# Attention scaled on VectorE behind both maxima, with transposed copies moved to ScalarE

## The chip, the cores and the metric

The kernel runs on one core of one Trainium2 chip. TensorE multiplies and transposes, VectorE (DVE in the rows), ScalarE (ACT) and GpSimd (POOL) work on rows of 128 partitions, SyncE (SP) issues most DMAs. Each engine takes its instructions in the order in which the program lists them, and waits at one whose inputs or buffers aren't ready. The metric is the device time of one execution in microseconds (us); less is better.

## What is computed

The reference runs attention and then two feed-forward blocks over its output, all in float32:

```
scores = q @ k.T / sqrt(64) + bias(i, j)       # 4 batches, 8 heads, 576 tokens, 64 per head
attn   = exp(scores - max(scores))             # rows of 576
attn   = attn / (sum(attn) + 1e-9)
x      = (attn @ v), heads side by side        # 2304 tokens x 512
x      = moe(x):  h = x @ w_in;  (h * cos(h)) @ w_out                       # width 2048
out    = moe2(x): rms norm, then (silu(xn @ w_gate) * (xn @ w_val)) @ w_out # width 1536
```

The bias is a small two-layer network of the distance of two tokens; it depends on the head and not on the batch.

## The kernel before

**Stages.** In the traced execution the first 64 us build the bias, attention follows to 357 us, and the two feed-forward blocks fill the rest. Their matrices arrive as 64-bit words and are taken apart on the chip.

**Units and steps.** Attention runs in 16 units: one batch and two heads each. A unit `u` has five steps `p`: steps 0 to 3 take 128 queries of both heads, step 4 the last 64 of both. The order in which `step(u, p)` writes its parts is the order of every engine's queue. A step holds:

- `qk(u, p)`: the scores into PSUM tiles `psS` (two buffers, so that it waits for the maxima of the step before).
- `softmax`: per head one VectorE instruction (L334, "maximum" below) that adds the bias, writes the sums to `e` and their extreme to `sm`, then ScalarE's exponential (L338), which also leaves the row sum. `sums` (L343, ScalarE) adds the 1e-9.
- `scale(u, p-1)`: the exponentials of the step before times the reciprocal of their sum: L350 is the reciprocal on VectorE, L353 one instruction of 128x576 for each head (one in step 4). After step 4's, L355 copies 64 columns on GpSimd.
- `tr(u, p-2)`: TensorE transposes the exponentials of two steps before into PSUM tiles `pt` (three buffers). For p < 4 there are two large tiles (four transposes, copied to `eT` by L367) and a small one (L371). Step 4 has one large and one small tile, copied by L377 and L380, L381.
- `av`: TensorE's products of `eT` with `v` (L393), for the unit before. They go to the one PSUM buffer `o`, which is emptied by L404 (ScalarE, the part `xh`) and L405 (VectorE, the remainder `xl`); the next `av` into `o` waits for L405. This happens at steps 0 and 2.

From unit 5 on the work on the first feed-forward matrices is mixed in: at step 1 L114 and L115 on VectorE, at step 4 L118 and L119 (a piece of a matrix is one such pair and the other), at step 0 L135 and L103 on ScalarE and L136 on GpSimd.

After the last unit, `scale(15, 4)` stands ahead of the first two items of the feed-forward part, inside which the last transposes and products run.

Of the kernel before, what the change touches and what calls it, by code (L numbers as in the profile page):

```python
# [11 lines left out]
ALU = mybir.AluOpType  # L12
# [3 lines left out]
B, H, S, D = 4, 8, 576, 64  # L16
# [29 lines left out]
def attn_moe(tc, qd, kd, vd, smallp, lrow, ident_d, wf1, wf2, rmsg, out):  # L46
    nc = tc.nc
# [137 lines left out]
    def load_bias(hp, j, eng=nc.sync):  # L185
        if hp >= NHP:
            return
        t = prep.tile([128, S], F32, tag=f"bias{j}", name=f"bias{j}", bufs=1)
        if j < 8:
            qt, hh = divmod(j, 2)  # L190
            eng.dma_start(
                t, bflat[2 * hp + hh, 128 * qt * ROW:128 * (qt + 1) * ROW]
                .rearrange("(p r) -> p r", r=ROW)[:, 16:16 + S])
        else:

            for p0, c0, c1, k0 in ((0, 0, S, 0), (64, 0, S - 64, 64), (64, S - 64, S, 0)):
                eng.dma_start(
                    t[p0:p0 + 64, c0:c1],
                    bflat[2 * hp + p0 // 64, 512 * ROW:576 * ROW]
                    .rearrange("(p r) -> p r", r=ROW)[:, 16 + k0:16 + k0 + c1 - c0])  # L200
        bias_t[j] = t
# [108 lines left out]
    def qk(u, p):  # L310


        kt, qt_ = kq[u]
        if p < 4:
            pss = [psB.tile([128, 2, 512], F32, tag="S", name="psS", bufs=2) for _ in range(2)]
            for x in range(2):
                for hh in range(2):
                    r = slice(64 * hh, 64 * hh + 64)
                    k0 = 64 - 64 * hh + 288 * x
                    nc.tensor.matmul(pss[hh][:, x, 0:288], qt_[r, 128 * p:128 * p + 128], kt[r, k0:k0 + 288],  # L320
                                     start=True, stop=True, tile_position=(64 * hh, 0))
            return pss
        ps = psB.tile([128, 2, 512], F32, tag="S", name="psS", bufs=2)
        for x in range(2):
            nc.tensor.matmul(ps[:, x, 0:288], qt_[:, 512:640], kt[:, 64 + 288 * x:352 + 288 * x], start=True, stop=True)  # L325
        return [ps]

    def softmax(u, j, ps):
        s_ = st[u]
        if j % 2 == 0:  # L330
            s_["e"][j // 2] = ep.tile([128, 2 * S], F32, tag="e", name="e", bufs=4)
        e2 = s_["e"][j // 2]
        e = e2[:, S * (j % 2):S * (j % 2) + S]
        nc.vector.tensor_tensor_reduce(  # L334
            out=e.rearrange("p (a b) -> p a b", a=2), in0=ps[:, :, 0:288],
            in1=bias_t[j].rearrange("p (a b) -> p a b", a=2),
            scale=-0.125, scalar=3.0e38, op0=ALU.add, op1=ALU.min, accum_out=s_["m"][:, j:j + 1])
        nc.scalar.activation(e, e, AF.Exp, bias=s_["m"][:, j:j + 1], scale=-1.0, accum_out=s_["sum"][:, j:j + 1])  # L338

    def sums(u, p):  # L340
        s_ = st[u]
        a, z = (2 * p, 2 * p + 2) if p < 4 else (8, 9)
        nc.scalar.activation(s_["sum"][:, a:z], s_["sum"][:, a:z], AF.Identity, bias=tiny)  # L343

    def scale(u, p):

        s_ = st[u]
        e2 = s_["e"][p]
        a, z = (2 * p, 2 * p + 2) if p < 4 else (8, 9)
        nc.vector.reciprocal(s_["r"][:, a:z], s_["sum"][:, a:z])  # L350
        for j in range(a, z):
            e = e2[:, S * (j % 2):S * (j % 2) + S]
            nc.gpsimd.tensor_tensor(e, e, s_["r"][:, j:j + 1].to_broadcast([128, S]), op=ALU.mult)  # L353
        if p == 4:
            nc.gpsimd.tensor_copy(e2[:, S:S + 64], e2[:, S - 64:S])  # L355

    def tr(u, p):
        s_ = st[u]
        e = s_["e"].pop(p)
        if p < 4:  # L360
            eT, q0 = (s_["eT0"], 128 * p) if p < 2 else (s_["eT1"], 128 * (p - 2))
            for c, ev in ((0, nc.scalar.copy), (2, nc.vector.tensor_copy)):
                pt = psA.tile([128, 512], F32, tag="tr", name="pt", bufs=3)
                for i in range(4):
                    k0 = 128 * (c + i // 2) + (S + 64) * (i % 2)
                    nc.tensor.transpose(pt[:, 128 * i:128 * i + 128], e[:, k0:k0 + 128], ident)  # L366
                ev(eT[:, 2 * c:2 * c + 4, q0:q0 + 128], pt.rearrange("p (c q) -> p c q", c=4))  # L367

            pt = psA.tile([128, 512], F32, tag="tr", name="pt", bufs=3)
            nc.tensor.transpose(pt[:, 0:128], e[:, 512:640], ident)  # L370
            nc.vector.tensor_copy(eT[:, 8, q0:q0 + 128], pt[:, 0:128])  # L371
        else:
            eT = s_["eT1"]
            pt = psA.tile([128, 512], F32, tag="tr", name="pt", bufs=3)
            for c in range(4):
                nc.tensor.transpose(pt[:, 128 * c:128 * c + 128], e[:, 128 * c:128 * c + 128], ident)
            nc.scalar.copy(eT[:, 0:8, 256:320], pt.rearrange("p (c q) -> p c q", c=8))  # L377
            pt = psA.tile([128, 512], F32, tag="tr", name="pt", bufs=3)
            nc.tensor.transpose(pt[:, 0:128], e[:, 512:640], ident)
            nc.vector.tensor_copy(eT[0:64, 8, 256:320], pt[0:64, 0:64])  # L380
            nc.vector.tensor_copy(eT[64:128, 8, 256:320], pt[64:128, 64:128])  # L381

    def av(u, half, cs):
        s_ = st[u]
        n = 256 if half == 0 else 320
        eT = s_["eT0"] if half == 0 else s_["eT1"]
        if cs[0] == 0:
            s_["o"] = psA.tile([128, 512], F32, tag="o", name="o", bufs=1)
        o = s_["o"]
        vt = vts[u]  # L390
        for c in cs:
            for hh in ((0, 1) if c % 2 else (1, 0)):
                nc.tensor.matmul(o[64 * hh:64 * hh + 64, 0:n], vt[:, c, 64 * hh:64 * hh + 64],  # L393
                                 eT[:, 2 * c + (hh if c < 4 else 0), :], start=(c == 0), stop=(c == 4),
                                 tile_position=(0, 64 * hh))

    def o_out(u, half):

        hp, b = divmod(u, 4)
        n = 256 if half == 0 else 320  # L400
        o = st[u]["o"][:, 0:n]
        t0 = b * S + 256 * half
        h, l = xh[:, hp, t0:t0 + n], xl[:, hp, t0:t0 + n]
        return [lambda: nc.scalar.copy(h, o),  # L404
                lambda: nc.vector.tensor_tensor(l, o, h.bitcast(F32), op=ALU.subtract)]  # L405

    def start_unit(u):
        hp, b = divmod(u, 4)
        vt = ap.tile([128, 5, 128], F32, tag="v", name="v", bufs=2)
        nc.sync.dma_start(vt, vd[b, hp])  # L410
        vts[u] = vt
        sm = ap.tile([128, 32], F32, tag="sm", name="sm", bufs=2)
        st[u] = {
            "m": sm[:, 0:9], "sum": sm[:, 10:19], "r": sm[:, 20:29], "e": {},
        }

    def step(u, p):
        hp, b = divmod(u, 4)
        if p == 0:
            start_unit(u)  # L420
        if u == 0 and p == 0:
            for j in (6, 7, 8):
                load_bias(0, j)
        outs = o_out(u - 2, 1) if p == 0 and u > 1 else o_out(u - 1, 0) if p == 2 and u > 0 else []
        for f in outs[:1]:
            f()
        pss = qk(u, p)
        if u or p:
            scale(*((u, p - 1) if p else (u - 1, 4)))
        for j, ps in enumerate(pss, 2 * p):  # L430
            softmax(u, j, ps)
            if b == 3:
                load_bias(hp + 1, j)
            if j % 2 == 0:
                for f in outs[1:]:
                    f()
        sums(u, p)
        if p == 2:
            st[u]["eT0"] = ap.tile([128, 9, 256], F32, tag="eT0", name="eT0", bufs=1)
        if p == 4:  # L440
            if u > 0:
                av(u - 1, 1, [4])
            st[u]["eT1"] = ap.tile([128, 9, 320], F32, tag="eT1", name="eT1", bufs=1)
        if p > 1:
            tr(u, p - 2)
        elif u > 0:
            tr(u - 1, p + 3)
        if u > 0 and p < 4:
            av(u - 1, *((0, [0, 1, 2]), (0, [3, 4]), (1, [0, 1]), (1, [2, 3]))[p])
        if p == 1 and u > 0:  # L450
            load_k(u + 1)
            load_q(u + 1)
        if u >= 4 and p in (1, 4):
            w_fill()
        if u >= 4 and p == 0:
            w_tick(lambda i: i < WA + WB)

    for u in range(16):
        for p in range(5):
            step(u, p)  # L460
# [329 lines left out]
```

## Time and profile before

| | |
|---|---|
| time, median of 3 runs (lowest to highest) | 1226.73 us (1226.02 to 1226.89) |
| time of the profiled execution | 1223.5 us |
| its span, first to last instruction | 1221.6 us |
| granted clock of TensorE, mean over the span | 0.997 |
| busy, share of the span | TensorE 96%, VectorE 69%, ScalarE 45%, GpSimd 40% |

The rows are those of the profiled execution, whose own time is 1.9 us above its span; it was 3.2 us faster than the median of the other runs. A busy time is the sum of an engine's instructions; "idle before" names what an engine waited for. Where two instructions of an engine overlap by their ends, their starts are further apart than nothing but nearer than their durations: starts are what a queue is counted by.

### The profile page before, as it was taken

What the parts mean: (1) busy time and instruction counts of PE and PEld (TensorE: products, weight loads), DVE (VectorE), ACT (ScalarE), POOL (GpSimd) and SP (SyncE); (2) the same over time, 40 slices, a digit from 0 to 9 for tenths busy, and PEclk for the clock granted to TensorE, in tenths of its full rate; (3) what the DMA queues carried; (4) which work ended last, traced back from release to release, by engine and by line L of the source; (5) the groups of instructions that cost most, each with busy time, mean ns of one, the idle gap of its engine ahead of it and who ended that gap; (6) DMA issues with size and microseconds to landing.
All of it is one profiled execution on the core that took longest, in us unless ns stands there. A gap on an engine that the chain in (4) does not pass through costs nothing.

```text
span 1221.6 us, 17077 instructions
## 1 busy us (share of the span) xinstructions
PE 1171.7 (96%) x6276; PEld 895.6 (73%) x6276; DVE 839.1 (69%) x1607; ACT 551.2 (45%) x1121; POOL 491.8 (40%) x471
## 2 busy tenths in 40 slices
PE   7889998888899999999999999999999999999998
PEld 2355555555567878888888887878888888888887
DVE  8866678777767869979888989687456255633232
ACT  6866776676655345444534545532232132212111
POOL 4155565665653225224424435674341232124111
PEclk9989999999999999999999999999999999999999
DMA  5922416143111101111110100121011111200012
GB/s 153 306 92 87 166 52 185 62 142 122 62 46 35 53 1 52 52 35 35 52 53 18 57 31 18 40 64 52 18 53 54 34 35 52 69 1 1 35 38 84
DMA packets 30323, 79.24 MB, mean 65 GB/s; under 512 B 3872, under 2 KB 4128, under 8 KB 30240
## 3 DMA queue, kind: packets, MB, share of 16 engines
q1 hardware_dynamic: 29616, 76.09, 19.7%
q0 software_dynamic: 480, 1.77, 0.6%
q8 instruction: 50, 0.82, 0.3%
q10 hardware_dynamic: 144, 0.29, 0.1%
q14 instruction: 33, 0.27, 0.1%
HBM read 62.52 MB, written 15.61 MB: 64 GB/s over the span
## 4 chain that ended last, share of the span: by engine, by line
PE 75%; DVE 15%; ACT 4%; issue 4%; DMA 1%; POOL 0%; DVEq 0%; ACTq 0%; POOLq 0%
PE y L499 24%; PE h L499 13%; PE hg L499 11%; PE hv L499 11%; PE o L393 6%; PE psS L320 4%; PE pt L366 3%; DVE e L334 3%; DVE ft L254 2%; PE psS L325 2%; PE psb L283 1%; DVE w L118 1%; DVE xl L405 1%; DVE w L114 1%; DVE t L539 1%
## 5 line engine op out<-in xcount | busy, mean ns | idle before, releaser
L499 PE MATMUL y<-g,wB 128*128 128x512 f32 (+1 forms) x960 | 213.6, 370 | 3.9 <-DVE yacc L594 1.7
L353 POOL TENSOR_TENSOR e<-e,sm 128x576 f32<-128x576 f32 x144 | 164.1, 1159 | 108.8 <-DVE sm L350 69.0
L547 POOL TENSOR_TENSOR g<-t,g 128x512 fp32r<-128x512 f32 (+1 forms) x80 | 97.5, 1219 | 245.8 <-ACT g L546 245.8
L499 PEld LDWEIGHTS y<-g,wB 128*128 128x128 f32 x960 | 167.5, 189 | 37.2 <-DVE yacc L594 3.0
L558 POOL TENSOR_TENSOR g<-t,g 128x512 fp32r<-128x512 f32 (+1 forms) x60 | 74.4, 1241 | 291.9 <-ACT g L557 291.9
L338 ACT ACTIVATE e<-e,sm 128x576 f32<-128x576 f32 x144 | 111.1, 772 | 93.7 <-DVE sm L334 91.6
L499 PE MATMUL h<-xh,wB 128*128 128x512 f32 (+1 forms) x480 | 145.8, 369 | 0.0
L499 PE MATMUL y<-wB,g 128*128 128x512 f32 x594 | 143.5, 389 | 0.0
L499 PE MATMUL hv<-xh,wB 128*128 128x512 f32 (+1 forms) x440 | 133.7, 369 | 0.0
L499 PE MATMUL hg<-xh,wB 128*128 128x512 f32 (+1 forms) x440 | 133.2, 368 | 0.4 <-DVE t L553 0.4
L334 DVE CUSTOM_DVE_ANT_0 e<-psS,bias 128x576 f32<-128x576 f32 x144 | 105.9, 753 | 39.6 <-PE psS L320 23.1
L553 DVE TENSOR_TENSOR t<-t,hg 128x512 f32<-128x512 f32 (+1 forms) x60 | 38.0, 633 | 137.4 <-ACT t L552 137.4
L499 PEld LDWEIGHTS y<-wB,g 128*128 128x128 f32 x594 | 110.8, 188 | 22.5
L393 PE MATMUL o<-eT,v 128*64 128x256 f32 (+1 forms) x640 | 94.6, 417 | 17.7 <-DVE xl L405 17.7
L552 ACT ACTIVATE t<-hg 128x512 f32<-128x512 f32 (+1 forms) x60 | 33.3, 556 | 167.9 <-PE hg L499 161.6
L557 ACT CAST g<-t 128x512 fp32r<-128x512 f32 (+1 forms) x60 | 34.7, 578 | 164.5 <-DVE t L556 164.5
L543 ACT ACTIVATE r<-r 128x512 f32<-128x512 f32 (+1 forms) x80 | 47.1, 589 | 127.4 <-DVE r L540 127.0
L499 PEld LDWEIGHTS h<-xh,wB 128*128 128x128 f32 x480 | 87.7, 188 | 16.2 <-POOL wB L136 0.7
L136 POOL TENSOR_TENSOR wB<-w,wB 128x512 fp32r<-128x512 f32 x61 | 85.5, 1408 | 19.6 <-ACT wB L135 19.6
L499 PEld LDWEIGHTS hg<-xh,wB 128*128 128x128 f32 x440 | 80.5, 188 | 15.0 <-DVE t L553 0.9
L499 PEld LDWEIGHTS hv<-xh,wB 128*128 128x128 f32 x440 | 80.6, 189 | 13.7
L499 PE MATMUL h<-xl,wB 128*128 128x512 f32 (+1 forms) x240 | 88.4, 368 | 0.0
(113 smaller groups left out, 2150.0 us busy)
## 6 DMA issues: line engine op xcount, KB each, us to landing
raw<-in_wf_dram SPq DMA_DIRECT2D x68, 512.0 KB, 3.6
bflat<-G SPq DMA_DIRECT2D x36, 295.5 KB, 4.0
bias<-bflat SPq DMA_DIRECT2D x26, 288.0 KB, 3.2
kt<-in_kd_dram SPq DMA_DIRECT2D x16, 320.0 KB, 4.6
qt<-in_qd_dram SPq DMA_DIRECT2D x16, 320.0 KB, 4.9
v<-in_vd_dram SPq DMA_DIRECT2D x16, 320.0 KB, 2.9
out_dram<-yacc SPq DMA_DIRECT2D x16, 256.0 KB, 2.1
bias<-bflat POOLq DMA_DIRECT2D x6, 288.0 KB, 5.6
```

The lines of the kernel that those rows point to most:

```text
L136: eng.tensor_tensor(t[:, 1, :], r, t[:, 0, :].bitcast(F32), op=ALU.subtract)
L320: nc.tensor.matmul(pss[hh][:, x, 0:288], qt_[r, 128 * p:128 * p + 128], kt[r, k0:k0 + 288], start=True, stop=True, tile_position=(64 * hh, 0))
L334: nc.vector.tensor_tensor_reduce(out=e.rearrange("p (a b) -> p a b", a=2), in0=ps[:, :, 0:288], in1=bias_t[j].rearrange("p (a b) -> p a b" ...
L338: nc.scalar.activation(e, e, AF.Exp, bias=s_["m"][:, j:j + 1], scale=-1.0, accum_out=s_["sum"][:, j:j + 1])
L353: nc.gpsimd.tensor_tensor(e, e, s_["r"][:, j:j + 1].to_broadcast([128, S]), op=ALU.mult)
L366: nc.tensor.transpose(pt[:, 128 * i:128 * i + 128], e[:, k0:k0 + 128], ident)
L393: nc.tensor.matmul(o[64 * hh:64 * hh + 64, 0:n], vt[:, c, 64 * hh:64 * hh + 64], eT[:, 2 * c + (hh if c < 4 else 0), :], start=(c == 0), s ...
L499: nc.tensor.matmul(ps, a, b_, start=(first and k == 0), stop=(last and k == tot - 1))
L543: nc.scalar.activation(r, r, AF.Abs)
L547: nc.gpsimd.tensor_tensor(g[:, 1, :tn], t, g[:, 0, :tn].bitcast(F32), op=ALU.subtract)
L553: nc.vector.tensor_tensor(t, t, pg, op=ALU.mult)
L558: nc.gpsimd.tensor_tensor(g[:, 1, :tn], t, g[:, 0, :tn].bitcast(F32), op=ALU.subtract)
```

## The change

It does three things. The two multiplications of `scale` go from GpSimd (`tensor_tensor` with the reciprocal broadcast) to VectorE (`tensor_scalar` with one value per partition). `scale(u, p-1)` is written behind both maxima of step `p` rather than ahead of them. And of the copies of transposed tiles, ScalarE takes the small one of every `tr` with p < 4 and the second large one of p = 2; in a unit that is four small ones and one of the four large ones that VectorE had.

```diff
@@ scale
         nc.vector.reciprocal(s_["r"][:, a:z], s_["sum"][:, a:z])
         for j in range(a, z):
             e = e2[:, S * (j % 2):S * (j % 2) + S]
-            nc.gpsimd.tensor_tensor(e, e, s_["r"][:, j:j + 1].to_broadcast([128, S]), op=ALU.mult)
+            nc.vector.tensor_scalar(e, e, s_["r"][:, j:j + 1], None, op0=ALU.mult)
@@ tr
-            for c, ev in ((0, nc.scalar.copy), (2, nc.vector.tensor_copy)):
+            for c, ev in ((0, nc.scalar.copy), (2, nc.scalar.copy if p == 2 else nc.vector.tensor_copy)):
...
             nc.tensor.transpose(pt[:, 0:128], e[:, 512:640], ident)
-            nc.vector.tensor_copy(eT[:, 8, q0:q0 + 128], pt[:, 0:128])
+            nc.scalar.copy(eT[:, 8, q0:q0 + 128], pt[:, 0:128])
@@ step
         pss = qk(u, p)
-        if u or p:
-            scale(*((u, p - 1) if p else (u - 1, 4)))
         for j, ps in enumerate(pss, 2 * p):
             softmax(u, j, ps)
...
         sums(u, p)
+        if u or p:
+            scale(*((u, p - 1) if p else (u - 1, 4)))
```

TensorE's order stays as it was. The first place is VectorE's queue from the two maxima of a step 1 to the first maximum of step 2, in a unit with L114 and L115 (`sm` holds extremes, sums and reciprocals, `w_` a piece of a matrix). Before:

```order
L334 ISA e,sm<-psS,bias_2840 128x576
L334 ISA sm 128x1
L334 ISA e,sm<-psS,bias_2844 128x576
L334 ISA sm 128x1
L380 COPY eT_2963<-pt 64x64
L381 COPY eT_2963<-pt 64x64
L114 TENSOR_SCALAR w_3026<-w_3026 128x512
L115 TENSOR_SCALAR w_3026<-w_3026 128x512
L350 RECIPROCAL sm<-sm 128x2
L334 ISA e,sm<-psS,bias_2880 128x576
L334 ISA sm 128x1
L405 TENSOR_TENSOR xl<-o,xh 128x256
```

And now:

```order
L334 ISA sm 128x1
L350 RECIPROCAL sm<-sm 128x2
L353 TENSOR_SCALAR e<-e,sm 128x576 x2
L380 COPY eT_2963<-pt 64x64
L381 COPY eT_2963<-pt 64x64
L114 TENSOR_SCALAR w_3026<-w_3026 128x512
L115 TENSOR_SCALAR w_3026<-w_3026 128x512
L334 ISA e,sm<-psS,bias_2877 128x576
L334 ISA sm 128x1
L405 TENSOR_TENSOR xl<-o,xh 128x256
```

The reciprocal that stood right ahead of step 2's first maximum was that of step 1; the one that now stands behind step 1's maxima is that of step 0, and two scalings follow it. The second place is VectorE's queue from step 4's maximum to the first maxima of the next unit:

```order
-L334 ISA e,sm<-psS,bias_2191 128x576
-L334 ISA sm 128x1
-L367 COPY eT_2571<-pt 128x4x128
-L371 COPY eT_2571<-pt 128x128
+L334 ISA e,sm<-psS,bias_2188 128x576
+L334 ISA sm 128x1
+L350 RECIPROCAL sm<-sm 128x2
+L353 TENSOR_SCALAR e<-e,sm 128x576 x2
 L118 SCALAR_TENSOR_TENSOR w_2448<-raw,w_2448 128x512
 L119 SCALAR_TENSOR_TENSOR w_2448<-raw,w_2448 128x512
-L350 RECIPROCAL sm<-sm 128x1
```

A large and a small copy went away ahead of L118, and a reciprocal with two scalings came. The third place is ScalarE's queue at the same point, from step 4's exponential to the maxima of the next unit:

```order
-L338 ACTIVATE e,sm<-e,sm 128x576
-L343 ACTIVATE sm<-sm,halfpi 128x1
+L371 COPY eT_2123<-pt 128x128
+L338 ACTIVATE e,sm<-e,sm 128x576
+L343 ACTIVATE sm<-sm,halfpi 128x1
+L367 COPY eT_2198<-pt 128x4x128 x2
+L371 COPY eT_2198<-pt 128x128
+L404 CAST xh<-o 128x320
```

Here one large and one small copy came in ahead of L404. GpSimd's queue loses the L353 instructions, so that L136 and L355 stand behind nothing but each other.

## Rows read from the trace of the kernel before

**Rows 1.** One stretch of attention: its length, busy time (instructions) by engine, granted clock, DMA.

```profile
104.00:122.00 18.00, 17.38 (x123) 10.65 (x120) 12.25 (x38) 12.35 (x32) 10.99 (x11) 1.00 0.29 90
```

**Rows 2.** Timeline of TensorE: step 4's scores in units 0, 2, 5, 6, 15; start, us, engine, line.

```profile
74.79 1.14 PE L325 MATMUL psS<-kt,qt 128*128 128x288 f32 x4
...
109.66 1.24 PE L325 MATMUL psS<-kt,qt 128*128 128x288 f32 x4
...
161.86 1.24 PE L325 MATMUL psS<-kt,qt 128*128 128x288 f32 x4
...
180.07 1.24 PE L325 MATMUL psS<-kt,qt 128*128 128x288 f32 x4
...
354.50 1.24 PE L325 MATMUL psS<-kt,qt 128*128 128x288 f32 x4
```

**Rows 3.** Timeline of unit 2, without matrix work, from step 1's scores into unit 3.

```profile
99.30 1.24 PE L320 MATMUL psS<-kt,qt 64*128 64x288 f32 x8
...
100.67 0.76 DVE L334 CUSTOM_DVE_ANT_0 e<-psS,bias 128x576 f32<-128x576 f32 x1 [0.77 <-PE psS L320]
...
102.03 0.21 DVE L380 COPY eT<-pt 64x64 f32<-64x64 f32 x1
...
103.45 0.17 DVE L350 RECIPROCAL sm<-sm 128x2 f32<-128x2 f32 x1 [0.97 <-ACT sm L343]
...
103.65 0.76 DVE L334 CUSTOM_DVE_ANT_0 e<-psS,bias 128x576 f32<-128x576 f32 x1
...
104.90 1.30 PE L393 MATMUL o<-eT,v 128*64 128x320 f32 x8 [0.34 <-DVE xl L405]
...
112.65 1.24 PE L320 MATMUL psS<-kt,qt 64*128 64x288 f32 x8
...
113.40 0.43 ACT L404 CAST xh<-o 128x320 fp32r<-128x320 f32 x1
...
115.25 1.51 PE L393 MATMUL o<-eT,v 128*64 128x256 f32 x12 [0.23 <-DVE xl L405]
```

**Rows 4.** Timeline of unit 10, with matrix work, from step 1's scores into unit 11.

```profile
246.05 1.24 PE L320 MATMUL psS<-kt,qt 64*128 64x288 f32 x8
...
247.53 1.28 POOL L136 TENSOR_TENSOR wB<-w,wB 128x512 fp32r<-128x512 f32 x1 [2.45 <-ACT wB L135]
...
249.28 0.92 DVE L114 TENSOR_SCALAR w<-w 128x512 f32<-128x512 f32 x1
...
250.23 1.25 DVE L115 TENSOR_SCALAR w<-w 128x512 int32<-128x512 int32 x1
...
252.83 1.30 PE L393 MATMUL o<-eT,v 128*64 128x320 f32 x8 [0.49 <-DVE xl L405]
...
261.38 0.68 DVE L118 SCALAR_TENSOR_TENSOR w<-raw,w 128x512 int32<-128x512 int32 x1
...
262.78 0.74 DVE L334 CUSTOM_DVE_ANT_0 e<-psS,bias 128x576 f32<-128x576 f32 x1
...
263.99 1.52 PE L393 MATMUL o<-eT,v 128*64 128x256 f32 x12 [1.03 <-DVE xl L405]
...
265.43 1.24 PE L320 MATMUL psS<-kt,qt 64*128 64x288 f32 x8
```

**Rows 5.** L114 from 68 to 200 us: durations in ns, least, median, most; starts.

```profile
L114 DVE TENSOR_SCALAR w<-w x3: 428/428/916, 154.7 to 191.1; 128x512 f32<-128x512 f32 x3
```

**Rows 6.** Group of a scaling of 128x576 by one value per partition, 0 to 68 us.

```profile
L254 DVE TENSOR_SCALAR ft<-L,nbp 128x576 f32<-128x576 f32 x7 | 3.2, 510 | 0.0
```

**Rows 7.** Groups from 68 to 357 us: count, busy us, mean ns, idle before them.

```profile
L353 POOL TENSOR_TENSOR e<-e,sm 128x576 f32<-128x576 f32 x143 | 163.0, 1159 | 106.6 <-DVE sm L350 66.7 <-PE pt L370 22.2 <-PE psS L320 16.8
...
L367 DVE COPY eT<-pt 128x512 f32<-128x512 f32 x62 | 42.6, 687 | 12.5 <-PE pt L366 12.5
...
L367 ACT COPY eT<-pt 128x512 f32<-128x512 f32 x62 | 35.1, 566 | 0.0
...
L371 DVE COPY eT<-pt 128x128 f32<-128x128 f32 x62 | 17.4, 280 | 0.0
```

## The prediction

> **What bounds the kernel now.** I read the page first (TensorE is busy for 96% of the span), then the stretches. In the feed-forward part TensorE is never without work for long, and the change leaves that part alone; in attention a stretch of 18.00 us holds 17.38 of TensorE and 12.25 of VectorE [rows 1]. That looks like a bound by TensorE, but a busy share hides how units differ, so next I took a period, from step 4's scores of one unit to those of the next [rows 2]. The five periods from 74.79 to 161.86 take 17.41 us each, the sixth 18.21, and the nine from 180.07 to 354.50 take 19.38 each. TensorE's work is the same in all of them: the 2 us more in a late period are waits, and they came with the matrix work.
>
> The timelines of an early and a late unit show where. Both begin with step 1's scores; I count from there. In unit 2 the first maximum of step 2 starts at 4.35 and the products that need `o` emptied at 5.60; until then VectorE had stood 0.97 us for ScalarE's sum [rows 3]. In unit 10 those products start at 6.78, because L114 and L115 took 0.92 and 1.25 us [rows 4]. The first two L114 took 0.428 us [rows 5]: they ran while GpSimd was idle, the slow ones beside its scaling. From these products to those of the next unit's step 0 it is 10.35 us in unit 2 and 11.16 in unit 10, where L118 and L119 hold up the next maximum. So 1.18 of the 2 us arise at the first place and 0.81 at the second. All of it is VectorE's queue, read as TensorE's wait for L405.
>
> **The change, part by part.**
>
> *A scaling on VectorE.* The trace has the same form on VectorE at the same width: 0.510 us [rows 6]. Starts are closer than durations (two maxima start 0.68 apart [rows 3] and take 0.76), so I count 0.43 in the queue and 0.51 for the last. The other end is one element per cycle, the pace of a maximum, 0.68; I take 0.43 since that row is the same instruction.
>
> *The reciprocal.* It stays, 0.20 in the queue with what follows it (103.45 to 103.65 [rows 3]), but it now takes sums that ScalarE finished a step ago, so its wait of 0.97 in step 2 goes. At this place the wait was cover for other work, and what stood in it now counts.
>
> *The first place without matrix work* [rows 3]. Two maxima from 1.37, 0.68 apart, end the queue at 2.73. Then the reciprocal 0.20, about 0.03 until its result can be read, two scalings 0.86, to 3.82; L380 and L381 0.44, to 4.26. Step 2's scores need the buffer of the second maximum, done at 1.37 + 0.68 + 0.76 = 2.81; a maximum starts 1.37 behind the issue of its scores, so not ahead of about 4.2, which I put at 4.27 for the hand-over. The maximum starts at 4.27 in place of 4.35 and the products, 1.25 behind it, at 5.52: **0.08 gained**. The two scalings just replace the wait. What is late next: the transposes of step 2 need the second scaling, done at 2.96 + 0.43 + 0.51 = 3.90, and TensorE gets to them behind step 2's scores, 2.81 + 1.24 = 4.05, so they don't wait.
>
> *The first place with matrix work* [rows 4]. L114 and L115 come on top. With GpSimd free they take 0.43 each [rows 5] and L115 reads L114's result, 0.86 together: maximum at 5.13, products at 6.38, against 6.78. **0.40 gained, and 0.86 more than without matrix work.**
>
> *The second place* [rows 3, 4]. From step 4's scores, VectorE's last maximum leaves the queue at 1.37 + 0.68 = 2.05; reciprocal and two scalings carry it to 3.14, L118 and L119 (1.40 from 261.38 to 262.78, with a reciprocal) to about 4.47. The next unit's first scores are issued 2.99 behind step 4's (109.66 to 112.65) and their maximum can start at 4.36. So 0.11 is lost there, in place of 0.81. **0.70 gained.** The two copies that left for ScalarE, 0.687 and 0.280 [rows 7], stood exactly here; without that part of the change the scalings would push the maximum out.
>
> *Copies on ScalarE.* A large one takes 0.566 there [rows 7]. For the small one there is no row; it lies between nothing and that 0.566, and I take 0.28, what it takes on VectorE. Per unit that is 1.7 us for an engine with 12.35 busy in 18 [rows 1]. The one place where it could bite is ahead of L404 of step 0, which now starts about 0.75 later: 0.75 behind the scores before (112.65 to 113.40 [rows 3]), 1.50 now, done at 1.93. L405 can start behind the first maximum, at 1.37 + 0.68 = 2.05. So it is covered by 0.12. At 0.566 for the small copy L405 would be 0.17 late in each period, 2.5 us over 15 periods; with a free copy nothing changes.
>
> *GpSimd.* The 143 scalings of 1.159 us [rows 7] go. Nobody waits for what stays there but the weights of the feed-forward part. L136 still runs at 1.48 to 2.76 of a late unit [rows 4]; with a small copy ahead of L135 on ScalarE it moves to about 1.7 to 3.0, while the first scaling wants to start at 2.96. They touch by some hundredths.
>
> *Ends.* The first unit loses two short waits of the reciprocal, from nothing to 0.3 us; I take nothing. After the last unit `scale(15, 4)` is covered by about 3 us of feed-forward products.
>
> **The sum.** Early period: 17.41 - 0.08 = 17.33. Late: 17.33 + 0.86 + 0.11 = 18.30. Four early periods give 0.3. The fifth holds the first L114 and L115, at 154.7 [rows 5], which hid in VectorE's wait of 0.97 and now no longer do: it loses 0.8. The sixth goes from 18.21 to 18.30 and loses 0.1. Nine late ones give 9 x 1.08 = 9.7. Together 9.1 us: the profiled execution would go from 1223.5 to 1214.4, and the median of the runs, 3.2 above it, from 1226.7 to 1217.6.
>
> **A rule that speaks against it.** First the rows: L114 and L115, 0.43 us alone, took 0.92 and 1.25 beside GpSimd's scaling [rows 4, 5], so a VectorE instruction of this kind can be held by GpSimd. The Trainium skill, page "SBUF — State Buffer", section "Who interferes with whom", says why: VectorE's two-port modes and GpSimd share one port pair, and whichever starts first holds it for its whole instruction while the other is blocked. By that rule a scaling that meets L136 would wait for its end, up to 1.28 us. The trace agrees so far as L114 goes; what it would make of the time is the first rival's, worked out from the rows.
>
> **Rivals.**
>
> *A scaling is held by L136.* Against it: they miss each other by my count. For it: the margin is hundredths, and a ScalarE queue that runs 0.6 later, as the added copies allow, would put L136 across both scalings. It decides when L136 starts behind 1.7. Each late period then loses 0.6 (half of 1.28) and the gain falls by about 5.5 to some 3.6: 1223.
>
> *A scaling runs at one element per cycle*, 0.68 in place of 0.43. Each pair costs 0.5 more at both places: early periods 17.83, late ones 19.30. Four lose 0.42, the fifth 1.3, the sixth 1.1, nine gain 0.08: 3.4 slower, 1230. Against it stands [rows 6].
>
> *VectorE's queue becomes the bound: the kernel is slower.* Nine scalings of 0.43 are 3.9 us per unit; the copies that leave are 0.69 + 4 x 0.28 = 1.8; so 2.1 more per unit, and 0.8 where L114 and L115 save 1.3. If VectorE's idle time is not to be filled, since each maximum still waits for scores and each copy for transposes, all of it lengthens the period: 6 x 2.1 + 9 x 0.8 = 20 us, 1247. It decides when scalings no longer lie within waits but push the next maximum past its scores in the early periods too. Against it: about 5.6 idle of 17.4 ((18.00 - 12.25) / 18 of the period [rows 1]), and my two walks find the scalings within it.
>
> *ScalarE is late with L404.* If the chain exponential, sum, two large copies and a small one runs 0.7 longer than I count, 15 periods lose that and nothing is gained: 1227.
>
> *The matrix work hides wholly.* Then late periods take 17.33 too: 10 more us, 1207.
>
> **Chances and range.** My forecast, 1213 to 1222: 0.62. L136 holds scalings: 0.10. One element per cycle: 0.08. VectorE's queue as the bound: 0.10. ScalarE late: 0.05. Matrix work hidden: 0.05. A measurement of this kernel can tell about 0.2%, 2.5 us, from no change. Faster by more than that are the first, the last and most of the second, 0.76; within it ScalarE's and the rest of L136's, 0.08; slower 0.16. The range 1209 to 1230 takes in the bounds of the scaling and of the small copy and leaves out the queue as the bound and the wholly hidden matrix work; the likeliest case alone is 1213 to 1222.
>
> **What would show it.** L353 on VectorE at about 0.51; L114 and L115 at 0.43 in all late units; periods of 17.3 early, 18.2 to 18.4 late, and the fifth no longer early; in a late unit the products of step 2 at 6.4 behind step 1's scores; idle of L350 for L343 gone. Wrong it would be if scalings take 0.7 or 1.2, if the early periods grow, or if TensorE's idle time is put down to ScalarE's copies.

## The result, and the profile after

The changed kernel takes 1214.24 us (median of 4 runs, 1213.45 to 1215.51) and the kernel before, beside it on the same chip, 1226.38 us (1224.84 to 1226.89): a ratio of 0.9904, 95% interval 0.9887 to 0.9921. It is 12.1 us faster by the medians; the forecast was 9.1 us, 1217.6. The two profiled executions differ by 10.05 us (1223.5 and 1213.45).

The page of the changed kernel, its first part: busy us, share of the span, instructions.

```profile
PE 1169.6 (97%) x6276; PEld 895.3 (74%) x6276; DVE 867.2 (72%) x1671; ACT 568.9 (47%) x1201; POOL 326.6 (27%) x327
```

Two stretches of attention in it, an early and a late one; the columns are those of [rows 1].

```profile
103.00:121.00 18.00, 17.71 (x125) 10.79 (x123) 14.99 (x43) 14.05 (x39) 0.24 (x1) 1.00 0.24 64
306.00:324.00 18.00, 16.71 (x118) 10.32 (x117) 16.06 (x44) 14.11 (x38) 1.52 (x2) 1.00 0.25 85
```

VectorE is fuller than before (14.99 in 18, against 12.25 in [rows 1]), GpSimd is nearly empty, and TensorE gets through more work in the early stretch (17.71 against 17.38). Step 4's scores of units 0 to 15 start at 75.55, 92.96, 110.07, 127.18, 144.29, 162.33, 180.44 and so on to 343.44. The periods are 17.41 (the first), 17.11 (three), 18.04 (the fifth) and 18.11 (the sixth and all later ones). Before, five took 17.41 on average, the sixth 18.21 and the later ones 19.38 [rows 2].

The timeline of the changed kernel from step 1's scores of unit 2 to the first products of unit 3, which answers to [rows 3]:

```profile
99.89 1.24 PE L320 MATMUL psS<-kt,qt 64*128 64x288 f32 x8
...
101.16 0.76 DVE L334 CUSTOM_DVE_ANT_0 e<-psS,bias 128x576 f32<-128x576 f32 x1 [0.87 <-PE psS L320]
...
104.06 0.76 DVE L334 CUSTOM_DVE_ANT_0 e<-psS,bias 128x576 f32<-128x576 f32 x1
...
105.31 1.30 PE L393 MATMUL o<-eT,v 128*64 128x320 f32 x8 [0.17 <-DVE xl L405]
...
113.06 1.24 PE L320 MATMUL psS<-kt,qt 64*128 64x288 f32 x8
114.33 0.76 DVE L334 CUSTOM_DVE_ANT_0 e<-psS,bias 128x576 f32<-128x576 f32 x1 [1.15 <-PE psS L320]
114.34 0.45 ACT L404 CAST xh<-o 128x320 fp32r<-128x320 f32 x1
...
115.55 1.52 PE L393 MATMUL o<-eT,v 128*64 128x256 f32 x12
```

And the same of a late unit, which answers to [rows 4]:

```profile
241.78 1.24 PE L320 MATMUL psS<-kt,qt 64*128 64x288 f32 x8
...
243.42 1.29 POOL L136 TENSOR_TENSOR wB<-w,wB 128x512 fp32r<-128x512 f32 x1 [1.44 <-ACT wB L135]
...
244.61 0.95 DVE L353 TENSOR_SCALAR e<-e,sm 128x576 f32<-128x576 f32 x2
...
245.96 0.43 DVE L114 TENSOR_SCALAR w<-w 128x512 f32<-128x512 f32 x1
...
246.42 0.43 DVE L115 TENSOR_SCALAR w<-w 128x512 int32<-128x512 int32 x1
...
246.88 0.76 DVE L334 CUSTOM_DVE_ANT_0 e<-psS,bias 128x576 f32<-128x576 f32 x1
...
248.12 1.30 PE L393 MATMUL o<-eT,v 128*64 128x320 f32 x8 [1.08 <-DVE xl L405]
...
252.88 1.24 PE L325 MATMUL psS<-kt,qt 128*128 128x288 f32 x4
...
257.23 0.75 DVE L334 CUSTOM_DVE_ANT_0 e<-psS,bias 128x576 f32<-128x576 f32 x1
...
258.45 1.52 PE L393 MATMUL o<-eT,v 128*64 128x256 f32 x12 [0.20 <-DVE xl L405]
```

Counted from step 1's scores, the products that need `o` emptied come at 5.42 in the early unit (105.31 - 99.89) and at 6.34 in the late one. From step 4's scores to the next unit's first products it is 5.48 (110.07 to 115.55) and 5.57 (252.88 to 258.45). So a late unit now loses 0.92 at the first place and 0.09 at the second, together the 1.00 by which its period is longer. The largest wait in it is still TensorE's 1.08 us for L405, behind L114 and L115.

### The profile page after: what moved, and what is told of

It reads as the page before. It is cut to its first block, busy times and chain, and to the rows that moved or that the text cites. A ratio compares the mean times of both kernels' runs of the same rounds, so it can differ in the third digit from the quotient of the medians.

```text
span 1211.7 us, 16932 instructions
## 1 busy us (share of the span) xinstructions
PE 1169.6 (97%) x6276; PEld 895.3 (74%) x6276; DVE 867.2 (72%) x1671; ACT 568.9 (47%) x1201; POOL 326.6 (27%) x327
## 4 chain that ended last, share of the span: by engine, by line
PE 74%; DVE 18%; ACT 3%; issue 3%; DMA 2%; POOL 0%; DVEq 0%; ACTq 0%; POOLq 0%
PE y L499 24%; PE h L499 13%; PE hg L499 11%; PE hv L499 11%; PE o L393 6%; PE psS L320 4%; DVE e L334 3%; PE pt L366 2%; DVE e L353 2%; DVE ft L254 2%; PE psS L325 1%; DMA bflat<-G 1%; DVE t L539 1%; DVE w L118 1%; DVE xl L405 1%
## 5 line engine op out<-in xcount | busy, mean ns | idle before, releaser
L334 DVE CUSTOM_DVE_ANT_0 e<-psS,bias 128x576 f32<-128x576 f32 x144 | 106.0, 754 | 40.3 <-PE psS L320 27.8
L136 POOL TENSOR_TENSOR wB<-w,wB 128x512 fp32r<-128x512 f32 x61 | 85.4, 1407 | 11.5 <-ACT wB L135 11.5
L320 PE MATMUL psS<-kt,qt 64*128 64x288 f32 x512 | 84.5, 442 | 2.9 <-DVE sm L334 2.6
```

The source lines that it names most:

```text
L136: eng.tensor_tensor(t[:, 1, :], r, t[:, 0, :].bitcast(F32), op=ALU.subtract)
L334: nc.vector.tensor_tensor_reduce(out=e.rearrange("p (a b) -> p a b", a=2), in0=ps[:, :, 0:288], in1=bias_t[j].rearrange("p (a b) -> p a b" ...
```

## The experiments

Each ran with the kernel before beside it on the same chip; ratios are to that. Lines are those of the changed kernel but where it is said otherwise. "Early" and "late" periods are those of units without and with matrix work.

### The parts of the change, one at a time

**The copies left where they were** (e2), the scalings on VectorE behind the maxima:

```diff
-            for c, ev in ((0, nc.scalar.copy), (2, nc.scalar.copy if p == 2 else nc.vector.tensor_copy)):
+            for c, ev in ((0, nc.scalar.copy), (2, nc.vector.tensor_copy)):
...
-            nc.scalar.copy(eT[:, 8, q0:q0 + 128], pt[:, 0:128])
+            nc.vector.tensor_copy(eT[:, 8, q0:q0 + 128], pt[:, 0:128])
```

> The changed kernel with all copies of transposed tiles back on VectorE where they were. Queue theory: only the large and the small copy ahead of L118 matter, about 0.8 us in each of ten late periods (18.1 to 18.9), while the early units hide them in VectorE's wait for step 0's scores (1.15 us there): 1222. Rival load theory (VectorE's total counts): 0.69 + 4 x 0.2 = 1.4 us in all 15 periods, 1235. Second rival (copies are free on either engine): 1214.

Measured: 1221.88 us, ratio 0.9974 [0.9962, 0.9987]. Early periods 17.11, as in the changed kernel; late ones 18.91 or 18.92 but for one of 19.05, against 18.11. The queue theory had both; the two rivals fell. The timeline of this kernel in a late unit shows that nearly all of the 0.81 lies at the second place:

```profile
257.08 1.24 PE L325 MATMUL psS<-kt,qt 128*128 128x288 f32 x4
...
260.90 0.68 DVE L118 SCALAR_TENSOR_TENSOR w<-raw,w 128x512 int32<-128x512 int32 x1
...
262.23 0.75 DVE L334 CUSTOM_DVE_ANT_0 e<-psS,bias 128x576 f32<-128x576 f32 x1
```

The next unit's maximum starts 5.15 behind step 4's scores, in the changed kernel 4.35 (252.88 to 257.23): 0.80 more, with the large and the small copy in front of L118.

**The copies alone** (e3): the kernel before, with the change to `tr` only.

> The kernel before with the copies moved to ScalarE, and nothing else. Queue theory: late periods lose the 0.7 us of the second place and keep the first, 19.4 to 18.7, early ones stay at 17.4: about 7 us less than before, 1219. Rival load theory: 1.4 us less in every period, 1206. Second rival (copies are free on either engine): 1226.

Measured: 1220.40 us, ratio 0.9963 [0.9950, 0.9976]; early periods 17.38, late 18.82, which is 0.56 less than before. The queue theory was nearest (1219); the late period stayed 0.1 above its 18.7. Of some 1225 us the two halves of the change give 3.2 and 4.5 by their ratios, and both together 11.8; counted in the periods of the profiled executions the halves give 3.5 and 5.6, and both 11.8. So the whole is more than its halves, by 2.7 to 4 us: scalings on VectorE fill the room that the copies leave.

**The scalings on VectorE ahead of the maxima** (e1), copies moved:

```diff
         pss = qk(u, p)
+        if u or p:
+            scale(*((u, p - 1) if p else (u - 1, 4)))
         for j, ps in enumerate(pss, 2 * p):
...
         sums(u, p)
-        if u or p:
-            scale(*((u, p - 1) if p else (u - 1, 4)))
```

> The changed kernel with the scaling on VectorE put back ahead of the maxima. Queue theory (the order counts because VectorE's queue ahead of step 2's first maximum holds up L405 and with it TensorE): the reciprocal waits for this step's predecessor's sum again and both scalings then stand between it and the maximum, so the products of step 2 come 1.1 us later in units without matrix work, which gives periods of about 18.4 there; in late units L114 and L115 fit into the wait for the sum, 18.6. Together some 10 us over the changed kernel, 1224. Rival (a scaling is needed only a step later, so its place in the step is free, and only its engine counts): 1214, periods as in the changed kernel.

Measured: 1232.95 us, ratio 1.0062 [1.0047, 1.0077], slower than before the change, and slower than either theory said. All periods behind the first are 18.87 or 18.88. The timeline of its unit 2, from step 1's scores:

```profile
103.80 1.24 PE L320 MATMUL psS<-kt,qt 64*128 64x288 f32 x8
...
108.08 0.17 DVE L350 RECIPROCAL sm<-sm 128x2 f32<-128x2 f32 x1 [0.98 <-ACT sm L343]
108.28 0.95 DVE L353 TENSOR_SCALAR e<-e,sm 128x576 f32<-128x576 f32 x2
109.26 0.76 DVE L334 CUSTOM_DVE_ANT_0 e<-psS,bias 128x576 f32<-128x576 f32 x1
...
110.51 1.30 PE L393 MATMUL o<-eT,v 128*64 128x320 f32 x8 [1.35 <-DVE xl L405]
```

Ahead of the maxima the reciprocal waits for ScalarE's sums of the step just ended (0.98 us here, 0.66 to 1.26 in every step of an early unit), and the scalings and the maximum come on top: step 2's first maximum is at 5.46, not 4.17. Late periods are no longer than early ones, since the matrix work fits into these waits: behind L114 and L115 the wait is 0.05 in place of 0.98, behind L118 and L119 nothing in place of 1.26. My theory had the direction and priced one such place in a period; it happens at every step.

**The scalings on GpSimd behind the maxima** (e4), copies moved:

```diff
-            nc.vector.tensor_scalar(e, e, s_["r"][:, j:j + 1], None, op0=ALU.mult)
+            nc.gpsimd.tensor_tensor(e, e, s_["r"][:, j:j + 1].to_broadcast([128, S]), op=ALU.mult)
```

> The changed kernel with the scalings on GpSimd as before, but behind the maxima. Queue theory: a pair takes 2.3 us from 2.9 on, so step 2's transposes wait until 5.2 and its products come at about 6.5 in early units (periods of 18.2); in late units L114 and L115 are held by GpSimd again (0.9 and 1.25 us) and products come at 6.9 (periods of 18.7). About 1224. Rival (order and copies make the gain, the engine does not count): 1214, L114 and L115 still long.

Measured: 1244.79 us, ratio 1.0153 [1.0129, 1.0178]; early periods 18.25, late ones mostly 20.26; in two of 21.3 the granted clock falls, to a mean of 0.72 from 204 to 210 us and from 327 to 333. The theory had the early period (18.2) and missed the late one (18.7). Timeline of this kernel, step 2 of an early unit:

```profile
105.84 1.24 PE L320 MATMUL psS<-kt,qt 64*128 64x288 f32 x8
...
105.99 2.25 POOL L353 TENSOR_TENSOR e<-e,sm 128x576 f32<-128x576 f32 x2 [2.28 <-PE o L393]
...
107.21 0.76 DVE L334 CUSTOM_DVE_ANT_0 e<-psS,bias 128x576 f32<-128x576 f32 x1 [1.00 <-POOL e L353]
...
108.30 0.98 PE L366 MATMUL pt<-ident,e 128*128 128x128 f32 x7 [0.78 <-POOL e L353]
```

Started behind the maxima, GpSimd's 2.25 us end after the transposes want the result: they stand 0.78 for it. The profile puts the maximum's wait of 1.00 down to GpSimd too, but that maximum does not read what is being scaled, and it starts 1.37 behind its scores (105.84 to 107.21), like the maxima of this kernel that wait for scores. In the late units L114 takes 1.19 us and L115 1.25, and L119 takes 1.52 in place of 0.69, which the theory had left out; that it makes up all of the 1.5 us it missed is not shown. With the copies on ScalarE the four ways of placing the scalings are now measured, as ratios to the kernel before: GpSimd ahead of the maxima 0.9963 (e3), VectorE ahead 1.0062 (e1), GpSimd behind 1.0153 (e4), VectorE behind 0.9904. The order helps only on the faster engine, and the faster engine only in this order.

**One of two scalings on GpSimd** (e6; here L354 is GpSimd's scaling and L356 VectorE's):

```diff
-            nc.vector.tensor_scalar(e, e, s_["r"][:, j:j + 1], None, op0=ALU.mult)
+            if j % 2:
+                nc.gpsimd.tensor_tensor(e, e, s_["r"][:, j:j + 1].to_broadcast([128, S]), op=ALU.mult)
+            else:
+                nc.vector.tensor_scalar(e, e, s_["r"][:, j:j + 1], None, op0=ALU.mult)
```

> The changed kernel, but one head's exponentials of each step (the second of the pair) are scaled on GpSimd, behind the maxima, as in the kernel in which GpSimd scaled both (1244.8 us); the last, single head of a unit stays on VectorE. If it was the length of GpSimd's two scalings (about 2.3 us together, and the maxima of the next step waiting for the buffer) that cost, half of it fits: GpSimd is done some 0.7 us after VectorE would be, the transposes wait for it, VectorE's own scaling or L114 meets a held port (0.9 to 1.1 us instead of 0.43), 1217 to 1228 us. If any scaling on GpSimd behind the maxima puts its whole 1.15 us between the maxima and the transposes, 1230 to 1240 us.

Measured: 1223.36 us, ratio 0.9981 [0.9971, 0.9990]; early periods 17.31 to 17.34 but for the first, late ones 18.88. Against the changed kernel a late period loses 0.77, an early one 0.23. In late units two instructions of the matrix work meet GpSimd, L114 and, at the second place, L118; the timeline:

```profile
249.14 1.39 POOL L354 TENSOR_TENSOR e<-e,sm 128x576 f32<-128x576 f32 x1
...
249.92 0.89 DVE L114 TENSOR_SCALAR w<-w 128x512 f32<-128x512 f32 x1
...
259.69 1.41 POOL L354 TENSOR_TENSOR e<-e,sm 128x576 f32<-128x576 f32 x1 [1.44 <-DVE sm L350]
...
260.01 1.64 DVE L118 SCALAR_TENSOR_TENSOR w<-raw,w 128x512 int32<-128x512 int32 x1
```

All eleven L114 took 0.89 here and 0.43 in the changed kernel; all eleven L118 took 1.64 here and 0.68 there. Most of the late units' loss is at L118: from step 4's scores to the next unit's step 1 a late unit is 0.60 us longer than an early one here (7.64 and 7.04), and 0.08 in the changed kernel (7.01 and 6.93). The expectation had named L114 and not L118. Its time held, the second expectation fell.

### Why the periods are shorter than forecast

The early period was forecast at 17.33 and is 17.11. In the changed kernel a maximum that waits for its scores starts 1.27 behind their issue (99.89 to 101.16, 113.06 to 114.33); before it was 1.37 (99.30 to 100.67 in [rows 3]). Before, GpSimd had written the buffer `e` that this maximum fills; now it has not. One buffer in five is an exception: step 4's, in which L355 still copies 64 columns on GpSimd. There are four such buffers, so the next unit's step 3 fills it again. The timeline of the changed kernel shows that copy and step 3 of unit 2:

```profile
99.82 0.24 POOL L355 COPY e<-e 128x64 f32<-128x64 f32 x1 [17.04 <-DVE e L353]
...
106.54 1.24 PE L320 MATMUL psS<-kt,qt 64*128 64x288 f32 x8
...
107.92 0.76 DVE L334 CUSTOM_DVE_ANT_0 e<-psS,bias 128x576 f32<-128x576 f32 x1 [0.42 <-PE psS L320]
```

It starts 1.38 behind its scores as before, although GpSimd was done with its buffer almost 8 us earlier. So do all step 3's: in units 1 to 15 these 15 maxima start 1.37 or 1.38 behind, the 35 others that wait for scores 1.27 or 1.28. To see whether GpSimd's part is the cause for the others too, it got a tiny read of every buffer (e7):

```diff
             nc.vector.tensor_scalar(e, e, s_["r"][:, j:j + 1], None, op0=ALU.mult)
+        nc.gpsimd.tensor_copy(s_["x"], e2[:, 0:1])
...
-            "m": sm[:, 0:9], "sum": sm[:, 10:19], "r": sm[:, 20:29], "e": {},
+            "m": sm[:, 0:9], "sum": sm[:, 10:19], "r": sm[:, 20:29], "x": sm[:, 31:32], "e": {},
```

> The changed kernel, with one copy of a single column by GpSimd out of the exponentials behind each scaling (79 short instructions, more work and not less), so that the next writer of the buffer, a first maximum, waits for GpSimd too, as it did before the change. The theory that the maximum starts 1.27 us behind its scores' first matmul instead of 1.37 because it waits for one engine and no longer for two: 1.37 comes back at the maxima that wait for scores, periods 17.3 to 17.4 early and 18.2 to 18.4 late, 1217 to 1219 us. The rival that the 0.10 us has another cause (what TensorE or VectorE did just before): 1.27 stays, 1213 to 1215 us.

Measured: 1217.77 us, ratio 0.9936 [0.9923, 0.9949]; periods of 17.30 to 17.33 early, but for the first, and 18.31 to 18.34 late. The timeline of this kernel, step 1 of unit 2:

```profile
101.45 1.24 PE L320 MATMUL psS<-kt,qt 64*128 64x288 f32 x8
...
102.83 0.76 DVE L334 CUSTOM_DVE_ANT_0 e<-psS,bias 128x576 f32<-128x576 f32 x1 [0.98 <-PE psS L320]
```

It is 1.38 again, though GpSimd's copy (0.19 to 0.41 us) was long done, and the forecast's periods of 17.33 and 18.30 come back.

### Matrix work put into waits

If a late unit's last 1.0 us is L114 and L115 (0.86) in the queue ahead of step 2's first maximum, then they are free where VectorE waits: 0.87 us ahead of step 1's first maximum, 1.15 ahead of step 0's. `w_fill` asks VectorE for the next pair; `w_tick` asks for L135, L136 and L103 and for the fetch of the next matrix. First only the step was changed, and `w_tick` begins a unit earlier (e5):

```diff
-        if u >= 4 and p in (1, 4):
+        if u >= 4 and p in (0, 4):
             w_fill()
-        if u >= 4 and p == 0:
+        if u >= 3 and p == 0:
             w_tick(lambda i: i < WA + WB)
```

> The changed kernel, with the matrix work of step 1 (the L136 that fetches, and the L114 and L115 that it brings) asked for in step 0, so that L114 and L115 stand ahead of the maximum of step 1 that waits 0.87 us for its scores, and not between the scalings and the maximum of step 2. The theory that a late unit's extra 1.0 us (18.11 against 17.11) is VectorE's 0.86 us of L114 and L115 standing in the queue ahead of step 2's first maximum: late units fall to 17.1 to 17.4, eleven of them by 0.7 to 1.0, so 1203 to 1206 us. The rival that the matrix work costs its load wherever it stands (on ScalarE's or TensorE's side, or as VectorE's wait is too short where it is put): 1212 to 1214 us, with another first maximum late by 0.8 instead.

Measured: 1206.77 us, ratio 0.9845 [0.9831, 0.9859]; late periods 17.48. The theory has the direction; the period is 0.1 above its range, and the time 0.8. The timeline of this kernel's late unit says why:

```profile
233.92 0.42 DVE L114 TENSOR_SCALAR w<-w 128x512 f32<-128x512 f32 x1
...
235.16 0.76 DVE L334 CUSTOM_DVE_ANT_0 e<-psS,bias 128x576 f32<-128x576 f32 x1 [0.36 <-PE psS L320]
...
237.84 1.24 PE L320 MATMUL psS<-kt,qt 64*128 64x288 f32 x8
...
238.15 0.68 DVE L118 SCALAR_TENSOR_TENSOR w<-raw,w 128x512 int32<-128x512 int32 x1
...
239.48 0.75 DVE L334 CUSTOM_DVE_ANT_0 e<-psS,bias 128x576 f32<-128x576 f32 x1
```

The pairs have changed places: L114 and L115 stand ahead of step 0's maximum, with 0.36 of its wait left over, and L118 and L119 ahead of step 1's, which starts at 1.64 and not at 1.27. The 0.37 lost there is the 0.37 by which the period is longer than 17.11. So next they were put the other way round, with one matrix more in advance (e8):

```diff
-        if u >= 4 and p in (1, 4):
+        if u >= 4 and p in (0, 4):
             w_fill()
-        if u >= 4 and p == 0:
+        if u >= 2 and p == 0:
             w_tick(lambda i: i < WA + WB)
+        if u >= 4 and p == 4:
+            w_dma()
+            wstate["dmad"] = wstate["dma"]
```

> The matrix work arranged by the waits that the traces show. In the run with L114 and L115 moved (1206.8 us) a late unit still took 17.48 us and not 17.11, because the pairs had changed places: L118 and L119 (1.36 us) stood in the wait of 0.87 us ahead of step 1's first maximum, and L114 and L115 (0.86 us) in the wait of 1.15 us ahead of step 0's. Here the kernel fetches one matrix further ahead, so that L114 and L115 stand ahead of step 1's first maximum and L118 and L119 ahead of step 0's, in every unit. Theory that each pair costs only what is longer than the wait it stands in: 0 at step 1, 0.2 at step 0, late units 17.2 to 17.35, twelve of them by 0.15 to 0.3 less than 17.48: 1203 to 1205.5 us. Rival (a pair costs something for standing there at all, a read of the product's low part behind it or the bookkeeping of another wait): 17.5 as before, 1206 to 1208 us.

Measured: 1206.89 us, ratio 0.9850 [0.9835, 0.9865]: nothing gained over e5, and late periods between 17.21 and 17.76. By time alone the rival would have won. The view of tile `raw`, the fetched words, in this kernel (durations in ns; then the idle time ahead of its users, us and times; last the time of a fetch) shows another cause:

```profile
L103 ACT ACTIVATE w<-raw x11: 686/696/712, 153.4 to 328.6; 128x512 f32<-128x512 f32 x11
its engine sat idle before it (us, times) until:
  DMA raw<-in_wf_dram: 4.0, 9
...
DMA to landing us min/median/max: 3.7/4.3/4.6
```

L103 now stood on ScalarE 4 us behind the issue of its fetch, with step 1's exponentials and L404 queued behind it. VectorE's L405 waited for L404 seven times, 2.6 us in all, and in the changed kernel never. The wait had moved from VectorE's queue to a DMA. Last, the same order on VectorE with L103 two steps later (e9):

```diff
-        if u >= 4 and p in (1, 4):
+        if u >= 4 and p in (0, 4):
             w_fill()
-        if u >= 4 and p == 0:
-            w_tick(lambda i: i < WA + WB)
+        if u >= 5 and p == 0 and wstate["split"] < min(wstate["convd"], WA + WB):
+            w_split()
+        if u >= 3 and p == 2:
+            w_abs()
+            wstate["absd"] = wstate["abs"]
+        if u >= 2 and p == 4:
+            while wstate["dma"] < wstate["conv"] + NRAW:
+                w_dma()
+            for k in ("dma", "conv", "split"):
+                wstate[k + "d"] = wstate[k]
```

> The same order on VectorE as in the run before it (1206.9 us), but the absolute value that ScalarE takes of a fetched matrix (L103) stands at the end of step 2 and no longer at the end of step 0. In that run L103 waited nine times for the fetch, 4.0 us in all (issue to landing 3.7 to 4.6 us), with step 1's exponentials and L404 behind it on ScalarE, and the late units came out uneven, 17.2 to 17.8. Theory that this wait took back what the order on VectorE gave: without it every late unit takes 17.2 to 17.35 us, 1202.5 to 1205 us. Rival (ScalarE's 0.7 us of L103 costs at step 2 too, or the pairs cost something wherever they stand): 17.45 or more, 1206 to 1208 us.

Measured: 1202.20 us, ratio 0.9810 [0.9793, 0.9827], the fastest version here and 0.3 below the range of the theory; late periods 17.18 or 17.19. The timeline of this kernel from step 1's scores of a late unit:

```profile
254.42 1.24 PE L320 MATMUL psS<-kt,qt 64*128 64x288 f32 x8
...
254.74 0.42 DVE L114 TENSOR_SCALAR w<-w 128x512 f32<-128x512 f32 x1
...
255.69 0.76 DVE L334 CUSTOM_DVE_ANT_0 e<-psS,bias 128x576 f32<-128x576 f32 x1
```

The maximum starts 1.27 behind its scores, as in a unit without matrix work. All but 0.08 of the 1.00 is gone, and L103 has no wait left.

## Why the prediction was right, step by step

**The bound.** VectorE's queue as TensorE's wait for L405, at two places, was right: e2 changes the second place alone and e5 and e9 move what stands at either, and the periods follow to 0.02 us. In e8 they did not, because of L103's wait.

**The scaling.** A pair takes 0.95 us from first start to last end (244.61 in the late unit); 0.43 + 0.51 was forecast. The rival of one element per cycle fell.

**The first place.** Forecast 5.52 and 6.38 for the products, measured 5.42 and 6.34. The reciprocal's wait of 0.97 was indeed replaced by the scalings, and L114 and L115 take 0.43 each. The term that was mis-sized is the 1.37 from a scores' issue to its maximum, which I carried over from before: it is 1.27 once GpSimd is out of that buffer, and e7 shows it. It counts once on the way to step 2's products (0.10) and once more from there to the next unit's (10.24 from 105.31 to 115.55, against 10.35 before): 0.2 in every period but the first.

**The second place.** Forecast: 0.11 lost in a late unit. Measured: 0.09 (5.57 against 5.48). That the copies make this possible was forecast, and e2 puts it at 0.81 in each late period. The rival that the matrix work hides wholly fell: late periods are 18.11, early ones 17.11.

**ScalarE.** L404 of step 0 was forecast to start 1.50 behind its scores and to be covered by 0.12; it starts at 1.28 (113.06 to 114.34). The small copy takes 0.27 there (0.28 estimated). ScalarE was not late.

**GpSimd.** L136 was put at 1.7 to 3.0 and runs from 1.64 to 2.93; the first scaling starts at 2.83. By the recorded times they overlap by 0.1 us. The view of line L353 in the changed kernel (durations in ns: least, median, most):

```profile
L353 DVE TENSOR_SCALAR e<-e,sm x144: 510/519/522, 68.1 to 348.0; 128x576 f32<-128x576 f32 x144
```

None of 144 was held, so this rival had no effect. The hold itself is real: in e6 L114 began 0.78 into GpSimd's scaling and ended 0.28 behind it, at 0.89 in place of 0.43. The Trainium skill, page "SBUF — State Buffer", section "Who interferes with whom", says that where one of VectorE's two-port modes meets GpSimd, whichever started first has the shared ports for its whole instruction. For L114 e6 agrees to within 0.15 us: begun anew at GpSimd's end (250.53) it would have ended at 250.96, and it ended at 250.81. Here the short overlap with L136 left no mark on the scaling.

**The sum.** Forecast: early periods 0.3 gained, the fifth 0.8 lost, the sixth 0.1 lost, nine late ones 9.7 gained. Measured: 0.9 gained (three of 0.3; the first hardly anything), 0.63 lost, 0.10 gained, and 9 x 1.27 = 11.4 gained: 11.8 in place of 9.1. The 2.7 more is the 0.2 of each period. In the first, step 0's scores start 3.48 behind step 4's (75.55 to 79.03) and in the others 2.99; why stays open. The spans differ by only 10.0, because two things outside the periods took 1.9 back in the profiled executions. Ahead of unit 0's step 4 it is 0.76 more, which is no more than executions of the same first units differ by (last section). Behind unit 15's step 4 it is 868.2 and not 867.1; in the six experiments that leave the matrix work in its steps it was 867.9 to 868.3, but for the 870.0 of e6, where the granted clock is 0.83 from 690 to 700 us. What makes the 1.1 us stays open.

So it is partly luck that 10.0 came out so near 9.1: one term was 2.7 too small, and 1.9 was not foreseen. The median missed by more, 1214.24 against 1217.6: 1.0 of the 3.4 is the profiled executions' own, and the rest is that I set the median 3.2 above the profiled execution, as before, where it lies 0.8 above (1213.45).

**The queue as the bound.** The rival on the other side, 1247, did not come, but e1 shows how near it was: the same scalings, written ahead of the maxima, make every early period 1.8 us longer than behind them (18.88 against 17.11).

## What to carry to other kernels

Work that moves to an engine with an in-order queue costs by the place where it is written, so look for the waits in that engine's timeline and put the work there: the same two scalings gained or lost with their place, and the same matrix work cost 1.0 us or 0.08 a unit. When such a move gains nothing, look at what its producers now wait for before giving up the theory; here it was a fetch of 4.3 us that no longer had its lead. Halves of a change that feed one queue should be tried together: alone they gave 3.2 and 4.5 us by their ratios, together 11.8.

## What had not been expected of the hardware

**A second engine to wait for costs VectorE 0.1 us even if it is long done.** A maximum waiting for scores starts 1.37 to 1.39 behind their issue where GpSimd had used its output buffer (before, e3, e4, e6, e7, and step 3 of the others) and 1.27 to 1.28 where it had not (the other steps of the changed kernel, e2, e5, e8 and e9), but for four of 477 in all. In the view of line L334 from 68 to 350 us there are 99 semaphore instructions of VectorE's queue with 139 maxima before, 48 with 141 after, and 97 with 142 in e7. That the extra instruction is what takes the 0.1 us is likely by this count and not shown by itself.

**When TensorE's clock rises at the start of attention differs between executions.** The granted clock of the changed kernel at the end of unit 0, in windows:

```profile
72.00:74.00 2.00, 2.00 (x9) 1.26 (x9) 0.92 (x2) 1.08 (x5) 0.00 (x0) 0.50 0.00 0
74.00:76.00 2.00, 2.00 (x15) 1.43 (x12) 1.39 (x5) 0.59 (x1) 0.00 (x0) 0.92 0.02 4
```

TensorE had been without work from 62 to 64 us; it then worked at 0.50, which is 1.2 GHz, until about 74.3 (0.92 on average in the window from 74 to 76), and at 2.4 GHz from there. Before, it rose at about 72. The first units of e5, e8 and e9 are those of the changed kernel. In e5 the window from 72 to 74 has 0.84, and step 4's scores of unit 0 start at 74.78, as before (74.79); in e8 and e9 that window has 0.56 and 0.67, and they start at 75.55 and 75.56. So the same instructions come out 0.78 apart, and the 0.76 us need not be of the change.
